# Attention and two expert stages in fp32 on one core: the q and k transposes of later units move from TensorE to VectorE

## The chip, the cores and the metric

The kernel runs on one core of one Trainium2 chip. Times are device microseconds of one execution; the number to predict is the median of the runs of the changed kernel. TensorE is PE, its weight loads PEld, VectorE is DVE, ScalarE ACT, GpSimd POOL; SP issues nearly all transfers.

## What is computed

```python
def _attn_ref(q, k, v, n_sink, window):        # (4, 8, 768, 64), 4 sinks, window 128
    scores = scale * np.matmul(q, k.transpose(0, 1, 3, 2))
    rel = pos[:, None] - pos[None, :]
    keep = (pos[None, :] < n_sink) | ((rel >= 0) & (rel < window))
    scores = np.where(keep, scores, -1e9)
    a = np.exp(scores - max); a = a / (sum + 1e-9)
    return np.matmul(a, v)

x = attn_out.transpose(0, 2, 1, 3).reshape(3072, 512)
x = ((x @ w1) * (x @ w2)) @ w3 @ w_out          # w's in float64, 1024 wide
e = argmax(x @ w_gate + bias[modality])         # 8 experts, top 1
out = gate[:, None] * (relu(x @ ew1[e]) @ ew2[e])
```

Everything is float32. Where the kernel needs nearly float32 accuracy from TensorE it splits an operand into a high part (rounded by ScalarE) and a low part (the difference) and adds three products.

## The kernel before

**Units and pairs.** The 3,072 tokens are 12 units of 256 tokens (4 batches, 3 units each; `c` is the unit's place in its batch). Attention works on one unit and one pair of heads at a time: 12 x 4 = 48 items, counted by `n`. On the 128 partitions lie the 2 x 64 head dimensions of the pair, or 128 tokens.

**One item of attention.** `a_load(n)` (L345) brings q and k, 128 tokens by 128 numbers each, in four transfers (L354). `a_tqk(n)` (L383) transposes the four 128x128 blocks on PE into the one PSUM bank of the pool `ps_t` (L392, L396). ScalarE writes the high parts from that bank, q to `qh` (L401) and k into a ring of three key blocks per pair (L402); one tick later `low_parts` writes the low parts, on DVE (L413, L415), for the first 8 items on PE and ACT. At the first unit of a batch POOL copies the four sink keys in front of each block of the ring (L421), so that a block is 4 + 128 columns wide. `a_scores(n, j)` (L427), for the two halves j of 128 queries, makes the scores in PSUM (L443), and DVE merges the two key blocks by a mask (L450 to L458) and takes the row maximum (L461); ACT takes the exponential with the row sum (L463) into `P`, which has the 4 sink columns ahead of the 128 window columns for each head. `norm` (L466) divides on DVE (L475). `a_sk` (L480) copies the sink columns of both heads side by side with ACT (L488); `a_skT` (L492) transposes them on PE (L499) into the one bank of `ps_x`. `a_pt` (L508) transposes the four window blocks of P on PE (L515), again into the bank of `ps_t`; ACT copies them out (L519, L521) and POOL keeps a triangle of each (L524). `a_pv` (L529) multiplies with v (L543, L546) and leaves the high part to ACT (L549), the low part to DVE (L554).

**The dense stages around it.** `moe1_stream` runs six groups of two units: per group eight pairs of 24 matmuls of 512 columns (L715) and pieces of six (L703) with the product of `w3` and `w_out`. Routing (`route`, L766) is DVE work, 16 reductions of 512 elements per unit (L776). The second expert stage follows attention, from about 620 us on.

**What sets the order.** `att_stream` (L562) yields steps, and `front` (L1005) takes them while it walks the dense stages; in each item the step order is:

```python
a_load(n + 2); a_scores(n, 0); yield
a_load_v(n); a_sk(n - 1); a_pt(n - 1); yield
a_tqk(n + 1); a_skT(n - 1); yield
a_scores(n, 1); yield
a_pv(n - 1); yield
```

From this program order a scheduler builds each engine's fixed queue at compile time. Each engine, SP too, then runs its queue in order, and an instruction that waits holds all behind it. The tiles qn and kn have two buffers each, so the load of item n + 2 waits for the last reader of item n.

Of the kernel before, what the change touches and what calls it, by code (L numbers as in the profile page):

```python
# [27 lines left out]
def attention_moe_moe_kernel(ctx, tc, q, k, v, w1, w2, w3, w_out, mod_id, w_gate, mod_bias, e_w1, e_w2, out,  # L28
                             n_sink, window, dbg=None):
    nc = tc.nc  # L30
# [17 lines left out]
    QDIV = float(D) ** 0.5  # L48
    FEW = 2 * NP if math.frexp(QDIV)[0] == 0.5 else 0
# [295 lines left out]
    def a_load(n):  # L345
        u, p = divmod(n, NP)
        b, c = divmod(u, NC)
        hs = slice(2 * p, 2 * p + 2)
        qn = att.tile([128, 2, 2 * D], F32, tag="qn", bufs=2, name="qn")
        kn = att.tile([128, 2, 2 * D], F32, tag="kn", bufs=2, name="kn")  # L350
        for src, dst in ((q, qn), (k, kn)):
            for j in range(2):
                s0 = c * UNIT + j * 128
                nc.sync.dma_start(out=dst[:, j].rearrange("p (h d) -> p h d", h=2),  # L354
                                  in_=src[b, hs, s0:s0 + 128, :].rearrange("h s d -> s h d"))
        nat[n] = (qn, kn)
# [26 lines left out]
    def a_tqk(n):  # L383
        u, p = divmod(n, NP)
        b, c = divmod(u, NC)
        qn, kn = nat.pop(n)
        if n < NP:
            ring.append(att.tile([128, 2, 3, KW], F32R, tag=f"ring{p}", bufs=1, name="ring"))
# [3 lines left out]
        tp = ps_t.tile([128, 4, 128], F32, tag="t", name="tqk")  # L392
        for x, src in enumerate((qn, kn)):
            for j in range(2):
                i = j if x == 0 or s0 < s1 else 1 - j
                nc.tensor.matmul(out=tp[:, 2 * x + i], lhsT=src[:, j], rhs=idf, is_transpose=True, start=(x + j == 0),  # L396
                                 stop=(x + j == 2), skip_group_check=True)
        qh = att.tile([128, 2, 128], F32R, tag="qh", bufs=2, name="qh")
        ql = att.tile([128, 2, 128], F32R, tag="ql", bufs=2, name="ql")
        scale = 1.0 / float(D) ** 0.5  # L400
        nc.scalar.activation(out=qh, in_=tp[:, 0:2], func=ACTF.Copy, scale=scale)  # L401
        nc.scalar.activation(out=kr[:, 0, blocks, NS:KW], in_=tp[:, 2:4], func=ACTF.Copy)  # L402

        def low_parts():
            if n < FEW:
                nc.tensor.matmul(out=tp[:, 0:2], lhsT=negq_r, rhs=qh, start=False, stop=True, skip_group_check=True)
                nc.tensor.matmul(out=tp[:, 2:4], lhsT=neg_r, rhs=kr[:, 0, blocks, NS:KW], start=False, stop=True,
                                 skip_group_check=True)
                nc.scalar.activation(out=ql, in_=tp[:, 0:2], func=ACTF.Copy, scale=scale)
# [3 lines left out]
            nc.vector.scalar_tensor_tensor(out=ql, in0=tp[:, 0:2], scalar=scale, in1=f32(qh), op0=ALU.mult,  # L413
                                           op1=ALU.subtract)
            nc.vector.tensor_tensor(out=kr[:, 1, blocks, NS:KW], in0=tp[:, 2:4], in1=f32(kr[:, 0, blocks, NS:KW]),  # L415
                                    op=ALU.subtract)
            sinks()

        def sinks():
            if c == 0:  # L420
                nc.gpsimd.tensor_copy(out=kr[:, :, :, 0:NS],  # L421
                                      in_=f32(kr[:, :, 0, NS:2 * NS]).unsqueeze(2).to_broadcast([128, 2, 3, NS]))

        stt["low", n] = defer(low_parts)
        stt["q", n] = (qh, ql)

    def a_scores(n, j):  # L427
# [12 lines left out]
        for i, (a, b_) in enumerate(((qh, 0), (ql, 0), (qh, 1))):  # L440
            for h in range(2):
                hp = slice(h * D, (h + 1) * D)
                nc.tensor.matmul(out=sp[:, h, 0:nk].rearrange("p (a b) -> p a b", b=KW), lhsT=a[hp, j, :],  # L443
                                 rhs=kr[hp, b_, blocks, :], start=(i == 0), stop=(i == 2))
        if j == 0:
            stt["p", n] = att.tile([128, 2, 2, KW], F32, tag="P", bufs=2, name="P")
        P = stt["p", n]
# [5 lines left out]
        else:  # L453
# [3 lines left out]
            if c == 0:  # L457
                nc.vector.copy_predicated(out=sp[:, :, 0:NS], mask=sk1_i.unsqueeze(1).to_broadcast([128, 2, NS]),  # L458
                                          data=negc.unsqueeze(1).to_broadcast([128, 2, NS]))
        lo = NS if blk0 else 0  # L460
        nc.vector.reduce_max(out=st[:, 0], in_=sp[:, :, lo:KW], axis=AXX, negate=True)  # L461
        for h in range(2):
            nc.scalar.activation(out=P[:, j, h, lo:KW], in_=sp[:, h, lo:KW], func=ACTF.Exp,  # L463
                                 bias=st[:, 0, h:h + 1], accum_out=st[:, 1, h:h + 1])

        def norm():  # L466
# [3 lines left out]
            if n < FEW:  # L470
                for h in range(2):
                    nc.scalar.activation(out=P[:, j, h, lo:KW], in_=P[:, j, h, lo:KW], func=ACTF.Copy,
                                         scale=r[:, h:h + 1])
                return
            nc.vector.tensor_tensor(out=P[:, j, :, lo:KW], in0=P[:, j, :, lo:KW],  # L475
                                    in1=r.unsqueeze(2).to_broadcast([128, 2, KW - lo]), op=ALU.mult)
# [3 lines left out]
    def a_sk(n):  # L480
        u, p = divmod(n, NP)
        b, c = divmod(u, NC)
        P = stt["p", n]
        for j in range(2):
            stt.pop(("norm", n, j))()
        j0 = 0 if c else 1
        skn = att.tile([128, 2, 2 * NS], F32, tag="skn", bufs=2, name="skn")
        nc.scalar.activation(out=skn[:, j0:2].rearrange("p j (h k) -> p j h k", h=2), in_=P[:, j0:2, :, 0:NS],  # L488
                             func=ACTF.Copy)
        stt["skn", n] = skn  # L490

    def a_skT(n):  # L492
        c = n // NP % NC
        skn = stt.pop(("skn", n))
# [3 lines left out]
        for j in range(0 if c else 1, 2):  # L498
            nc.tensor.transpose(out=xp[0:2 * NS, 1, j * 128:(j + 1) * 128], in_=skn[:, j], identity=idf)  # L499
# [8 lines left out]
    def a_pt(n):  # L508
        u, p = divmod(n, NP)
        b, c = divmod(u, NC)  # L510
        P = stt.pop(("p", n))
        tp = ps_t.tile([128, 4, 128], F32, tag="t", name="pt")
        for j in range(2):
            for h in range(2):
                nc.tensor.transpose(out=tp[:, 2 * j + h, :], in_=P[:, j, h, NS:KW], identity=idf)  # L515
# [13 lines left out]
    def a_pv(n):  # L529
# [25 lines left out]
        stt.pop(("q", n))  # L555
# [6 lines left out]
    def att_stream():  # L562
# [5 lines left out]
        for n in range(NN):  # L568
# [18 lines left out]
        a_sk(NN - 1); a_pt(NN - 1); yield  # L587
        a_skT(NN - 1)
# [641 lines left out]
```

## Time and profile before

| | us |
|---|---|
| runs | 990.64, 990.67, 991.0 (median 990.67) |
| the profiled execution's own time | 990.5 |
| its span, first to last instruction | 988.5 |
| busy: PE, DVE, ACT, POOL | 955.5, 634.0, 442.1, 161.0 |

An engine is busy while one of its instructions runs; durations of matmuls overlap, so the distance between two starts is what a matmul takes of PE, not its duration. A busy PE is not PE at its peak. The profile's line numbers are those of the code above.

### The profile page before, as it was taken

Reading aid. Unit: us, or ns where it says so; the run is one execution under the profiler, and the core shown is the slowest. Engines: PE = TensorE matmul, PEld = TensorE weight load, DVE = VectorE, ACT = ScalarE, POOL = GpSimd, SP = SyncE. Lnnn points to the kernel's source line nnn. Section 1 sums busy time; section 2 is a strip of 40 time slices with the busy share of each in tenths; the row PEclk is TensorE's granted clock in tenths of the full one; section 3 lists DMA queues with packets and bytes.
Section 4 is the critical chain, followed back from the end, with each engine's and each line's share of the span. In section 5 each row is a group of like instructions: output and inputs, shape, how many; then the busy total and the mean of one; then the engine's idle time right before and its main releaser. Section 6 shows DMA issues by size and latency. Waiting matters only on the chain. (4 is left out here: it accounts for less than half of the span.)

```text
span 988.5 us, 15433 instructions
## 1 busy us (share of the span) xinstructions
PE 955.5 (97%) x5000; PEld 728.4 (74%) x5000; DVE 634.0 (64%) x1913; ACT 442.1 (45%) x1266; POOL 161.0 (16%) x237
## 2 busy tenths in 40 slices
PE   4899999999999999999999999999999999999995
PEld 3667777767776777677767776787888888888884
DVE  7956994599449953995499538939934373443432
ACT  3687763454335433553355335413434334433433
POOL 1111110111112111111111111123130312211010
PEclk9899999999999999999999999999999999999998
DMA  8754724122212221221022210422455465444331
GB/s 255 237 159 137 224 73 124 29 54 62 46 28 46 64 46 25 51 73 42 19 54 69 47 23 10 138 76 55 141 180 115 150 78 167 149 144 135 106 121 51
DMA packets 125409, 93.99 MB, mean 95 GB/s; under 512 B 96711, under 2 KB 105159, under 8 KB 125200
## 3 DMA queue, kind: packets, MB, share of 16 engines
q1 hardware_dynamic: 120560, 80.12, 30.2%
q0 software_dynamic: 4768, 12.88, 4.1%
q8 instruction: 40, 0.66, 0.3%
q14 instruction: 41, 0.34, 0.2%
HBM read 80.14 MB, written 13.09 MB: 94 GB/s over the span
## 5 line engine op out<-in xcount | busy, mean ns | idle before, releaser
L715 PE MATMUL ab<-xb,wab 128*128 128x512 f32 x1152 | 288.5, 397 | 0.0
L715 PEld LDWEIGHTS ab<-xb,wab 128*128 128x128 f32 x1152 | 209.9, 188 | 44.6 <-DVE xb L554 0.2
L961 PE MATMUL x<-w 128*128 128x512 f32 x600 | 141.0, 392 | 0.0
L776 DVE CUSTOM_DVE_ANT_0 junk<-rows,wgb 128x512 bf16<-128x512 f32 x192 | 137.0, 714 | 1.9 <-ACT rows L763 0.5
L703 PE MATMUL x2p<-w3o,gh 128*128 128x512 f32 x384 | 130.1, 416 | 0.5 <-ACT gh L692 0.5
L961 PEld LDWEIGHTS x<-w 128*128 128x128 f32 x600 | 111.6, 188 | 23.1 <-DVE w L201 0.4
L524 POOL TENSOR_SCALAR_AFFINE_SELECT ptp<-ptf 128x512 f32<-128x512 f32 (+1 forms) x96 | 63.6, 687 | 344.9 <-ACT ptf L519 344.9
L463 ACT ACTIVATE P<-sp,st 128x132 f32<-128x132 f32 (+1 forms) x192 | 69.2, 366 | 67.6 <-DVE st L461 62.4
L201 DVE TENSOR_TENSOR w<-wst,w 128x512 fp32r<-128x512 f32 x112 | 71.3, 685 | 10.8 <-ACT w L200 10.8
L703 PEld LDWEIGHTS x2p<-w3o,gh 128*128 128x128 f32 x384 | 65.7, 189 | 16.2 <-ACT gh L692 2.8
L703 PE MATMUL x2p<-w3o,gl 128*128 128x512 f32 x192 | 76.5, 399 | 0.0
L722 DVE TENSOR_TENSOR g<-ab,bs 128x256 f32<-128x256 f32 x48 | 20.3, 423 | 85.6 <-PE tqk L396 49.0
L924 PE MATMUL ab<-w,w 128*128 128x512 f32 x288 | 74.9, 395 | 0.0
L928 DVE SCALAR_TENSOR_TENSOR w<-ab,w 128x512 fp32r<-128x512 f32 x48 | 33.1, 690 | 64.4 <-ACT w L927 64.2
L924 PE MATMUL ab<-w 128*128 128x512 f32 x288 | 73.6, 391 | 0.0
L692 ACT ACTIVATE gh<-g 128x256 fp32r<-128x256 f32 x96 | 39.7, 415 | 73.8 <-DVE g L722 55.7
L200 ACT ACTIVATE w<-wst 128x512 fp32r<-128x512 f32 x112 | 63.3, 628 | 7.4 <-DMA wst<-in_moe_w_dram 7.2
L443 PE MATMUL sp<-ring,qh 64*128 64x264 f32 (+1 forms) x384 | 62.7, 331 | 3.6 <-ACT P L463 3.5
L924 PEld LDWEIGHTS ab<-w,w 128*128 128x128 f32 x288 | 53.9, 188 | 12.4
L924 PEld LDWEIGHTS ab<-w 128*128 128x128 f32 x288 | 54.1, 188 | 12.1
L443 PEld LDWEIGHTS sp<-ring,qh 64*128 64x128 f32 x384 | 37.5, 185 | 34.6 <-issue 15.1
L927 ACT ACTIVATE w<-ab 128x512 fp32r<-128x512 f32 x48 | 28.7, 597 | 71.8 <-PE ab L924 71.4
(201 smaller groups left out, 1430.8 us busy)
## 6 DMA issues: line engine op xcount, KB each, us to landing
wst<-in_moe_w_dram SPq DMA_DIRECT2D x56, 512.0 KB
f64st<-in_moe_w_dram SPq DMA_DIRECT2D x32, 512.0 KB
vn<-in_v_dram SPq DMA_DIRECT2D x128, 64.0 KB
xs<-rows SPq DMA_DIRECT2D x12, 513.0 KB
qn<-in_q_dram SPq DMA_DIRECT2D x96, 64.0 KB
kn<-in_k_dram SPq DMA_DIRECT2D x96, 64.0 KB
f64st<-in_moe_w_out_dram SPq DMA_DIRECT2D x8, 512.0 KB
wgb<-wgt SPq DMA_DIRECT2D x1, 2048.0 KB
```

The source lines that it names most:

```text
L200: nc.scalar.activation(out=hi, in_=src, func=ACTF.Copy)
L201: lo_eng.tensor_tensor(out=lo, in0=src, in1=f32(hi), op=ALU.subtract)
L443: nc.tensor.matmul(out=sp[:, h, 0:nk].rearrange("p (a b) -> p a b", b=KW), lhsT=a[hp, j, :], rhs=kr[hp, b_, blocks, :], start=(i == 0), st ...
L463: nc.scalar.activation(out=P[:, j, h, lo:KW], in_=sp[:, h, lo:KW], func=ACTF.Exp, bias=st[:, 0, h:h + 1], accum_out=st[:, 1, h:h + 1])
L524: nc.gpsimd.affine_select(out=parts[:, a, i0:2].rearrange("p j h q -> p (j h) q"), in_=full[:, 2 * i0:4], pattern=[[0, 4 - 2 * i0], [sign, ...
L692: nc.scalar.activation(out=gh, in_=g, func=ACTF.Copy)
L703: nc.tensor.matmul(out=x2p[t], lhsT=a[:, sl], rhs=b_, start=(f == 0 and i == 0), stop=(f == KF - 1 and i == 2))
L715: nc.tensor.matmul(out=bank[nm].rearrange("p (u t) -> p u t", u=2), lhsT=a, rhs=b_, start=(kk == 0 and i == 0), stop=(kk == KD - 1 and i = ...
L776: nc.vector.tensor_tensor_reduce(out=junk, in0=rows[:, t, 0:DM], in1=wgb[0][:, e, :], scale=1.0, scalar=0.0, op0=ALU.mult, op1=ALU.add, ac ...
L924: nc.tensor.matmul(out=hp, lhsT=a[:, fs], rhs=b_, start=(kk == 0 and i == 0), stop=(kk == KD - 1 and i == 2))
L928: nc.vector.scalar_tensor_tensor(out=h[:, 1], in0=hp, scalar=0.0, in1=f32(h[:, 0]), op0=ALU.max, op1=ALU.subtract)
L961: nc.tensor.matmul(out=op, lhsT=a[:, ts], rhs=b_, start=(f == 0 and i == 0), stop=(f == KF - 1 and i == 2))
```

## The change

Items from n = 8 on (`BY_PE`) load q and k in blocks of 32 tokens by 32 dimensions: eight transfers instead of four, each to 32 partitions, in runs of 128 bytes instead of 256. One instruction of DVE, in place, turns all 32x32 blocks of q and k, which gives what PE's four transposes gave; ACT and DVE then read the parts from that tile in SBUF and not from PSUM. The first 8 items still use PE.

The ring's blocks get the sink keys a second time at their end (two copies on POOL instead of one). Head 0 reads window then sinks, head 1 sinks then window, so that in P the sinks of both heads lie side by side in columns 128 to 135. The ACT copy of the sinks goes, the sinks are transposed straight out of P, and this step comes right behind the transposes of P.

```diff
-        qn = att.tile([128, 2, 2 * D], F32, tag="qn", bufs=2, name="qn")
-        kn = att.tile([128, 2, 2 * D], F32, tag="kn", bufs=2, name="kn")
...
+        qk = att.tile([128, 2, UNIT], F32, tag="qk", bufs=2, name="qk")
+        for x, src in enumerate((q, k)):
+            if n < BY_PE:
...
+            for g in range(4):
+                h, d0 = 2 * p + g // 2, g % 2 * 32
+                nc.sync.dma_start(out=qk[g * 32:(g + 1) * 32, x].rearrange("p (b i) -> p b i", i=32),
+                                  in_=src[b, h, c * UNIT:(c + 1) * UNIT, d0:d0 + 32].rearrange("(b s) i -> s b i", s=32))
...
+        else:
+            nc.vector.transpose(out=qk.rearrange("p x s -> p (x s)"), in_=qk.rearrange("p x s -> p (x s)"))
+            qt, kt = (qk[:, x].rearrange("p (j s) -> p j s", j=2) for x in range(2))
+            if s0 > s1:
+                kt = kt[:, ::-1]
...
-        nc.scalar.activation(out=qh, in_=tp[:, 0:2], func=ACTF.Copy, scale=scale)
-        nc.scalar.activation(out=kr[:, 0, blocks, NS:KW], in_=tp[:, 2:4], func=ACTF.Copy)
+        nc.scalar.activation(out=qh, in_=qt, func=ACTF.Copy, scale=scale)
+        nc.scalar.activation(out=kr[:, 0, blocks, NS:KW], in_=kt, func=ACTF.Copy)
...
-                nc.gpsimd.tensor_copy(out=kr[:, :, :, 0:NS],
-                                      in_=f32(kr[:, :, 0, NS:2 * NS]).unsqueeze(2).to_broadcast([128, 2, 3, NS]))
+                for s0 in (0, KW):
+                    nc.gpsimd.tensor_copy(out=kr[:, :, :, s0:s0 + NS],
+                                          in_=f32(kr[:, :, 0, NS:2 * NS]).unsqueeze(2).to_broadcast([128, 2, 3, NS]))
...
+                c0 = (1 - h) * NS
+                nc.tensor.matmul(out=sp[:, h, c0:c0 + nk].rearrange("p (a b) -> p a b", b=KW), lhsT=a[hp, j, :],
+                                 rhs=kr[hp, b_, blocks, c0:c0 + KW], start=(i == 0), stop=(i == 2))
...
+            nc.tensor.transpose(out=xp[0:2 * NS, 1, j * 128:(j + 1) * 128], in_=P[:, j, 128:128 + 2 * NS], identity=idf)
...
-                a_sk(n - 1); a_pt(n - 1); yield
+                a_pt(n - 1); a_skT(n - 1); yield
             if n + 1 < NN:
                 a_tqk(n + 1)
-            if n:
-                a_skT(n - 1)
```

Where the queues change: first PE, in a stretch at the end of a dense group (about 301 to 304 us before). Line numbers below are each kernel's own. Before:

```order
L515 MATMUL pt<-idf,P 128x128 x4
L703 MATMUL x2p<-w3o,gh 128x512 x2
L703 MATMUL x2p<-w3o,gl 128x512
L703 MATMUL x2p<-w3o,gh 128x512 x2
L703 MATMUL x2p<-w3o,gl 128x512
L396 MATMUL tqk<-idf,qn 128x128 x2
L396 MATMUL tqk<-idf,kn 128x128 x2
L499 MATMUL xp<-idf,skn 8x128 x2
L703 MATMUL x2p<-w3o,gh 128x512 x2
L443 MATMUL sp<-ring,qh 128x264 x2
```

The same place with the change:

```order
L527 MATMUL pt<-idf,P 128x128 x4
L712 MATMUL x2p<-w3o,gh 128x512
L509 MATMUL xp<-idf,P 8x128 x2
L712 MATMUL x2p<-w3o,gh 128x512
L712 MATMUL x2p<-w3o,gl 128x512
L712 MATMUL x2p<-w3o,gh 128x512 x2
L712 MATMUL x2p<-w3o,gl 128x512
L712 MATMUL x2p<-w3o,gh 128x512 x2
L458 MATMUL sp<-ring,qh 128x264 x2
```

The four transposes of q and k are gone, and those of the sinks stand one matmul behind the transposes of P.

Then DVE, between the products g of the first and second column block of the next group. Before:

```order
L468 TENSOR_SCALAR st<-st 128x2
L776 ISA junk,lg<-rows,wgb 128x512
L776 ISA lg 128x1
L469 RECIPROCAL st<-st 128x2
L776 ISA junk,lg<-rows,wgb 128x512
L776 ISA lg 128x1
L475 TENSOR_TENSOR P<-P,st 128x2x128
L776 ISA junk,lg<-rows,wgb 128x512
```

With the change:

```order
L497 TENSOR_TENSOR P<-P,st 128x264
L796 CAST oh<-wk 128x16
L802 RECIPROCAL sm<-sm 128x2
L407 STREAM_TRANSPOSE qk<-qk 128x512
L470 COPY_PREDICATED sp<-past_i,negc 128x2x124
L803 COPY rows<-sm 128x2
L785 ISA junk,lg<-rows,wgb 128x512
L785 ISA lg 128x1
L484 TENSOR_REDUCE st<-sp 128x2
L428 TENSOR_TENSOR ring<-qk,ring 128x2x128
```

A block transpose (L407) has come in. From the last g of the group before to its first g the queue of DVE held 22 routing reductions (junk) and now holds 19 and three block transposes; in the next three blocks there were 7, 3 and 0 reductions and are 4, 7 and 2.

Last SP, at one of the routing stores xs; the brackets are the semaphores waited for. Before:

```order
L795 DMA xs<-rows 128x2x513 [waits DMAHW1_49,DVE_49,Activation_49]
L354 DMA qn<-in_q_dram 128x2x64 [waits DMAHW2_49,PE_49]
L354 DMA qn<-in_q_dram 128x2x64 [waits DMAHW3_49]
L354 DMA kn<-in_k_dram 128x2x64 [waits DMAHW4_49,PE_49]
L354 DMA kn<-in_k_dram 128x2x64 [waits DMAHW5_49]
L365 DMA vn<-in_v_dram 128x2x64 [waits DMAHW6_49,PE_49]
```

With the change:

```order
L804 DMA xs<-rows 128x2x513 [waits DMAHW1_49,DVE_49]
L360 DMA qk<-in_q_dram 32x8x32 [waits DMAHW2_49,DVE_49]
L360 DMA qk<-in_q_dram 32x8x32 [waits DMAHW3_49]
L360 DMA qk<-in_q_dram 32x8x32 [waits DMAHW4_49]
L360 DMA qk<-in_q_dram 32x8x32 [waits DMAHW5_49]
L360 DMA qk<-in_k_dram 32x8x32 [waits DMAHW6_49]
```

The load of q and k now waits for DVE (the low parts) where it waited for PE (the transposes), and has eight issues.

## Rows read from the trace of the kernel before

**Rows 1.** Page, parts 1 and 2: busy us (share) xinstructions, then forty slices of the span.

```profile
PE 955.5 (97%) x5000; PEld 728.4 (74%) x5000; DVE 634.0 (64%) x1913; ACT 442.1 (45%) x1266; POOL 161.0 (16%) x237
...
DVE  7956994599449953995499538939934373443432
PEclk9899999999999999999999999999999999999998
```

**Rows 2.** Windows of 50 us: length, busy us (x instructions) by engine, granted clock, DMA share, GB/s.

```profile
250.00:300.00 50.00, 50.00 (x274) 37.73 (x272) 23.63 (x78) 18.19 (x58) 7.81 (x10) 1.00 0.16 25
300.00:350.00 50.00, 48.71 (x289) 34.72 (x288) 47.17 (x168) 25.90 (x95) 8.85 (x14) 1.00 0.24 57
```

**Rows 3.** Timeline of PE alone: start us, duration, engine, line, operation, output and inputs.

```profile
302.79 0.38 PE L396 MATMUL tqk<-idf,qn 128*128 128x128 f32 x2
303.01 0.38 PE L396 MATMUL tqk<-idf,kn 128*128 128x128 f32 x2
303.22 0.38 PE L499 MATMUL xp<-idf,skn 128*8 128x128 f32 x2
303.36 0.71 PE L703 MATMUL x2p<-w3o,gh 128*128 128x512 f32 x2
...
311.06 0.44 PE L396 MATMUL tqk<-idf,qn 128*128 128x128 f32 x2
...
393.08 0.38 PE L396 MATMUL tqk<-idf,qn 128*128 128x128 f32 x2
...
393.51 0.38 PE L499 MATMUL xp<-idf,skn 128*8 128x128 f32 x2
```

**Rows 4.** Groups with shapes apart, q and k transposes on PE: x count | busy us, mean ns | idle.

```profile
L396 PE MATMUL tqk<-idf,qn 128*128 128x128 f32 x96 | 19.8, 285 | 0.1
L396 PE MATMUL tqk<-idf,kn 128*128 128x128 f32 x96 | 18.7, 276 | 0.0
```

**Rows 5.** Waits of PE, its weight loads, from 100 to 620 us: total us, times, longest.

```profile
PEld tqk L396 <- ACT ptf L519: 2.6, 8, 0.5
...
PEld tqk L396 <- ACT ptp L521: 1.8, 5, 0.4
```

**Rows 6.** Groups with shapes apart, VectorE: a block transpose and others of its width.

```profile
L752 DVE STREAM_TRANSPOSE wgst<-wgst 32x512 f32<-32x512 f32 x1 | 0.7, 692 | 0.0
...
L201 DVE TENSOR_TENSOR w<-wst,w 128x512 fp32r<-128x512 f32 x112 | 71.3, 685 | 10.8 <-ACT w L200 10.8
...
L776 DVE CUSTOM_DVE_ANT_0 junk<-rows,wgb 128x512 bf16<-128x512 f32 x192 | 137.0, 714 | 1.9 <-ACT rows L763 0.5
```

**Rows 7.** Windows of 10 us, columns as in Rows 2.

```profile
320.00:330.00 10.00, 9.00 (x57) 5.86 (x58) 9.88 (x40) 6.05 (x25) 2.20 (x4) 1.00 0.19 43
330.00:340.00 10.00, 10.00 (x57) 7.61 (x56) 9.87 (x37) 4.71 (x18) 1.61 (x3) 1.00 0.32 93
```

**Rows 8.** Timeline of VectorE: the low part of k for the unit transposed at 302.79.

```profile
306.79 0.42 DVE L415 TENSOR_TENSOR ring<-tqk,ring 128x256 fp32r<-128x256 f32 x1
```

**Rows 9.** Groups with shapes apart: ScalarE by source, its sink copies, and the copy of sink keys.

```profile
L401 ACT ACTIVATE qh<-tqk 128x256 fp32r<-128x256 f32 x48 | 18.4, 384 | 44.2 <-PE tqk L396 43.6
...
L692 ACT ACTIVATE gh<-g 128x256 fp32r<-128x256 f32 x96 | 39.7, 415 | 73.8 <-DVE g L722 55.7 <-PE x2p L703 16.8 <-DVE gl L693 1.0
...
L488 ACT ACTIVATE skn<-P 128x16 f32<-128x16 f32 x32 | 6.9, 215 | 21.1 <-DVE P L475 18.9 <-DVE wk L783 1.6 <-DVE cwork L163 0.6
...
L421 POOL CAST ring<-ring 128x24 fp32r<-128x24 f32 x16 | 4.1, 254 | 66.2 <-ACT ring L410 30.8 <-DVE ring L415 13.8 <-DVE sp L458 12.3
```

**Rows 10.** DMA view from 250 to 300 us, SP timeline there, SP waits of the span.

```profile
q1 hardware_dynamic: 4923, 1.20, 14.9%
...
257.14 0.89 SPq L354 DMA_DIRECT2D qn<-in_q_dram  x2
258.12 0.94 SPq L354 DMA_DIRECT2D kn<-in_k_dram  x2
...
SPq L795 <- DVE rows L794: 47.3, 9, 23.7
```

More of the change, by code (lines that the diff above doesn't have):

```diff
@@ L391, in a_tqk @@
         blocks = slice(s0, s1 + 1) if s0 < s1 else slice(s1, s0 + 1, s0 - s1)
[L392 to L397, printed above, removed]
+        if n < BY_PE:
+            tp = ps_t.tile([128, 4, 128], F32, tag="t", name="tqk")
+            for x in range(2):
+                for j in range(2):
+                    i = j if x == 0 or s0 < s1 else 1 - j
+                    nc.tensor.matmul(out=tp[:, 2 * x + i], lhsT=qk[:, x, j * 128:(j + 1) * 128], rhs=idf, is_transpose=True,
+                                     start=(x + j == 0), stop=(x + j == 2), skip_group_check=True)
+            qt, kt = tp[:, 0:2], tp[:, 2:4]
+        else:
[3 more added lines that the diff above has]
+                kt = kt[:, ::-1]
         qh = att.tile([128, 2, 128], F32R, tag="qh", bufs=2, name="qh")
@@ L442, in a_scores, with both @@
                 hp = slice(h * D, (h + 1) * D)
-                nc.tensor.matmul(out=sp[:, h, 0:nk].rearrange("p (a b) -> p a b", b=KW), lhsT=a[hp, j, :],
-                                 rhs=kr[hp, b_, blocks, :], start=(i == 0), stop=(i == 2))
+                c0 = (1 - h) * NS
+                nc.tensor.matmul(out=sp[:, h, c0:c0 + nk].rearrange("p (a b) -> p a b", b=KW), lhsT=a[hp, j, :],
+                                 rhs=kr[hp, b_, blocks, c0:c0 + KW], start=(i == 0), stop=(i == 2))
         if j == 0:
-            stt["p", n] = att.tile([128, 2, 2, KW], F32, tag="P", bufs=2, name="P")
-        P = stt["p", n]
+            stt["p", n] = att.tile([128, 2, 2 * (KW + NS)], F32, tag="P", bufs=2, name="P")
+        P = stt["p", n][:, j]
+        flat = sp.rearrange("p h c -> p (h c)")
+        def both(first, step, n_):
+            return flat[:, first:first + 2 * step].rearrange("p (h c) -> p h c", h=2)[:, :, 0:n_]
         st = att.tile([128, 3, 2], F32, tag="st", bufs=6, name="st")
@@ L471, in norm @@
                 for h in range(2):
[L472 to L473 removed]
+                    nc.scalar.activation(out=rows[:, h], in_=rows[:, h], func=ACTF.Copy, scale=r[:, h:h + 1])
                 return
[L475 to L476 removed]
+            nc.vector.tensor_tensor(out=rows, in0=rows, in1=r.unsqueeze(2).to_broadcast([128, 2, KW - (NS if blk0 else 0)]),
+                                    op=ALU.mult)
         stt["norm", n, j] = defer(norm)
[L480 to L490, printed above, removed]
     def a_skT(n):
         c = n // NP % NC
[L494 removed]
+        P = stt["p", n]
         xp = ps_x.tile([128, 2, 256], F32, tag="x", name="xp")
@@ L510, in a_pt @@
         b, c = divmod(u, NC)
-        P = stt.pop(("p", n))
+        P = stt["p", n]
+        for j in range(2):
+            stt.pop(("norm", n, j))()
         tp = ps_t.tile([128, 4, 128], F32, tag="t", name="pt")
@@ L514, in a_pt @@
             for h in range(2):
[L515 removed]
+                nc.tensor.transpose(out=tp[:, 2 * j + h, :], in_=P[:, j, h * (KW + NS):h * (KW + NS) + 128], identity=idf)
         full = att.tile([128, 4, 128], F32, tag="ptf", bufs=1, name="ptf")
```

38 lines of the change are left out of this document (20 added, 18 removed).

## The prediction

> **What bounds the kernel now.** The first view is the page. PE is busy for 97% of the span and its slices read 9 nearly throughout, while VectorE is at 64% with slices that swing between 3 and 9 [rows 1]. The granted clock is full (the 2.4 GHz level) from the second slice on, so no time is to be had from the clock. A share of 64% is an average, so the second view is the windows: in the window of 250 to 300 us PE is busy for all 50.00 us and VectorE for 23.63, and in the next one PE for 48.71 and VectorE for 47.17 [rows 2]. The kernel alternates between stretches where PE alone sets the pace and stretches, around the end of each dense group, where VectorE has almost no room either: 9.88 and 9.87 of 10 us [rows 7]. There are five such ends with attention in them between 190 and 610 us, one per group. So what comes off PE is gained one for one in the first kind of stretch; in the second kind it is gained only if VectorE does not become later. That is the question here, since the change takes work from PE and gives work to VectorE.
>
> **What it removes.** From item 8 on, 40 items, PE loses four transposes each, 160 in all. What one set costs is read from starts, since durations overlap: from the first q transpose at 302.79 to the sink transposes that follow them at 303.22 is 0.43 us, and from 393.08 to 393.51 again 0.43 [rows 3]. So 40 x 0.43 = **17.2 us** off PE. The other way to price it is the busy time of the group, 19.8 + 18.7 = 38.5 us for 192 transposes [rows 4], 160/192 of which is 32 us; but that counts the drain of each set, under which the next matmuls have begun (the second pair lasts 0.38 us, yet the next row starts 0.21 after it). I take the 17.2 and keep the 32 as the far end of the gain.
>
> The transposes also share one PSUM bank with those of P, and PE waited for ACT to empty it: 2.6 us in 8 waits and 1.8 us in 5 between 100 and 620 us, where all 40 items lie [rows 5]. With q and k out of this bank that is **4.4 us** less. Below, the end is nothing, if the matmul that moves up waits for something else that is late.
>
> On this the Trainium skill, page "VectorE: DVE Perf Modes", speaks twice. Its section "The three transpose paths" gives 390 ns for a 128x128 bf16 block on TensorE and 311 on VectorE; by an estimate from its 390, 40 sets of four would be 62 us of PE, and the time about 924. The rows, 0.43 us for four in a row, decide against that figure. Its section "Rules for kernel authors" would leave a 128x128 transpose on TensorE where PSUM will do, which speaks against the change; what that would cost here is the first rival below.
>
> **What it adds to VectorE.** 40 block transposes, 512 columns on 128 partitions. The trace has one on 32 partitions, 692 ns; other instructions of 512 columns on 128 partitions take 685 to 714 [rows 6], so partitions do not seem to matter. 40 x 0.69 = 27.7 us, on an engine with 64% busy. On the path I cost them at nothing, and the cover is this: the routing reductions (0.714 us each, [rows 6]) are needed only much later and fill the queue wherever there is room. In the queue printed above the saturated stretch loses three reductions (2.1 us) and gains three block transposes (2.1 us), and the reductions come back in the next three column blocks, in the part of the group where VectorE was idle for half the time [rows 2]. If that cover is gone, it costs 5 ends x 3 x 0.69 = 10 us.
>
> **What is hidden anyway.** ACT loses 48 sink copies of some 0.21 us, and pays for reading 80 operands from SBUF: 415 ns against 384 from PSUM [rows 9], 2.5 us in all; at 45% busy both are nothing. POOL copies sink keys twice, 16 x 0.254 us = 4.1 us more [rows 9], in front of the scores of a batch's first unit; I take 0 and keep 4 as the bad end. Scores, maximum, exponential and division keep their sizes.
>
> **What is moved.** The sink transposes follow those of P almost at once, so the bank that they write must already be free: the low part of the item before (DVE, L554) must have been read from it. Before, four q and k transposes and four more matmuls stood between. No row shows this wait on the new place. Below it is nothing; above it is the longest wait for the other bank, 0.5 us [rows 5], in each of some 20 items near group ends, 10 us. Nearest is that bank's average, 4.4/13 = 0.34 us; in one of four such items that is 5 x 0.34 = **1.7 us**, which I take. Behind the waiting transposes all of PE's queue stands.
>
> **The loads.** Eight issues at 0.46 us each (four took 0.89 + 0.94 us, [rows 10]) are 3.7 us of SP. From 250 to 300 us 4,923 packets, nearly all of 256 bytes, took 14.9% of 16 engines, 24 ns each [rows 10]. An item's 2,048 packets of 128 bytes are then between 1.5 us (by bytes) and 6.2 (twice as long each); at 24 ns, 3.1 us. Issue and packets one after the other are 6.8 us. The buffer is now free only after the low parts: 307.2 for the item transposed at 302.79 [rows 3, 8], 4.4 us later than before. Items follow at 8.3 us there (302.79, 311.06, [rows 3]), so from that moment to the block transpose two items on are 2 x 8.3 - 4.4 = 12.1 us. It fits, and costs nothing.
>
> **The sum**, against the profiled execution (990.5 us, span 988.5, that is 0.17 below the median of the runs): 990.5 - 17.2 - 4.4 + 1.7 = 970.6, in round numbers **970.5 us**.
>
> **Rivals.**
> *VectorE sets the pace at the group ends.* Then the four or so items of each end (20 of 40) save PE work without shortening anything, and half of the bank waits stay: 990.5 - 8.6 - 2.2 = about 980. For it: 9.88 of 10 us [rows 7]. Against it: three reductions leave just there, and PE was busy for 48.71 of 50 us in the same window. If the reductions that leave are not those that were in the way, the 10 us above are added, and it is 990, no change.
>
> *The block transpose waits for its load, and VectorE with it* (the side that ends slower). The load now waits for VectorE, and a store of routing rows, itself waiting for VectorE, stands ahead of the loads on SP: such stores held SP for 47.3 us in 9 waits, 23.7 us at the longest [rows 10]. A block transpose at the head of VectorE's queue then stops maxima, divisions and low parts, and PE next. It decides where the time from the store's release to the block transpose is under some 7 us. At 1 us lost by PE per item the sum is 970.5 + 40 = about 1,010, and above half a microsecond per item the kernel is slower than before. Against it are the 12.1 us, and that SP's long waits were for buffers that nobody needed yet. The Trainium skill, "DMA: Bandwidth & Descriptors", section "Specifications", says that transfers under 512 bytes are read, modified and written and miss the line rate, which speaks for it; the runs before, of 256 bytes, were under this limit too, and nothing here shows the step from 256 to 128.
>
> *Nothing is gained*, because the matmuls that move up wait for the exponentials of the scores ahead of them: about 990. Against it: PE has dense matmuls between in most places.
>
> *More is gained*: with PE's drains counted (the 32 us), about 960.
>
> **How the numbers follow.** Forecast 0.70 (its own range 964 to 979); VectorE's pace 0.14 (975 to 988); late loads 0.07; nothing 0.05; more 0.04. Under 962 lies little of the last, over 984 the second half of the late cases, so 962 to 984 holds a bit over 8 in 10. A measurement can tell 0.2%, 2 us, from no change: faster is 0.70 + 0.04 + 0.13 = 0.87, the same 0.05, slower 0.08.
>
> **What would show it.** Right: no q and k transposes after the first 8 items; PE busy about 18 us less with the idle time near what it was; block transposes of about 0.69 us; VectorE near 660 us busy, with the reductions spread over more column blocks; SP's waits for VectorE without a wait of VectorE for the loads. Wrong: waits of VectorE for q or k transfers, PE's sink transposes waiting for the low part of the item before, or windows at the group ends where VectorE is full and PE idle for over 2 us.

## The result and the profile after

The changed kernel takes **975.64 us** (median of 975.31, 975.55, 975.73 and 977.43) against 990.67 before, a ratio of 0.985 with a 95% interval of 0.9838 to 0.9862. The forecast was 970.5 with a range of 962 to 984, so the sign and the range hold, and 15.0 us were gained where 20 were forecast. Three quarters of the forecast came; the experiments ask where the other 5 us are.

The page of the changed kernel, parts 1 and 2, answers to [rows 1]:

```profile
PE 932.9 (96%) x4840; PEld 709.7 (73%) x4840; DVE 651.8 (67%) x1953; ACT 440.5 (45%) x1218; POOL 167.2 (17%) x253
...
DVE  7956996699659964896599649929934374333422
...
PEclk9999999999999999999999999999999999999998
```

PE has exactly the 160 instructions less, and 22.6 us less of busy time. The span fell by only 14.7 us (988.5 to 973.8), so PE now stands idle for 40.9 us where it was 33.0: **7.9 us of new idle time**. The clock is at its 2.4 GHz level as before, and has no part in it.

The windows say where the idle time is (length, busy us by engine, clock, DMA share, GB/s; the first four answer to [rows 2, 7]):

```profile
250.00:300.00 50.00, 49.84 (x276) 37.00 (x276) 28.25 (x94) 19.93 (x60) 9.91 (x14) 1.00 0.21 39
300.00:350.00 50.00, 45.87 (x269) 33.12 (x265) 47.66 (x173) 24.20 (x86) 7.93 (x14) 1.00 0.27 53
320.00:330.00 10.00, 8.97 (x53) 6.38 (x54) 9.57 (x43) 4.95 (x18) 2.19 (x4) 1.00 0.27 44
330.00:340.00 10.00, 10.00 (x54) 7.54 (x54) 9.90 (x33) 4.09 (x17) 1.50 (x2) 1.00 0.35 83
290.00:350.00 60.00, 55.72 (x324) 39.24 (x322) 56.07 (x201) 30.00 (x105) 9.58 (x16) 1.00 0.27 52
```

The last line of these has this counterpart in the kernel before:

```profile
290.00:350.00 60.00, 58.71 (x341) 41.41 (x339) 54.09 (x188) 30.78 (x109) 10.07 (x16) 1.00 0.22 52
```

In the long stretch of this dense group PE is full, or nearly so, in both. Around the group's end, 290 to 350 us, PE was idle for 1.29 us and is now idle for 4.28, and VectorE went from 54.09 to 56.07 of 60. The five ends are not alike. Counted from the copy of a group's eighth column block to that of the next group's second, PE's idle time grew by 0.3, 1.6, 1.4, 0.3 and 0.3 us; another 1.4 us lie behind the second end, at 349 us, and 1.0 in the first group. The moved work itself is as forecast (groups of VectorE from 90 to 610 us: xcount | busy us, mean ns | idle before, and what ended it):

```profile
L785 DVE CUSTOM_DVE_ANT_0 junk<-rows,wgb 128x512 bf16<-128x512 f32 x148 | 105.5, 713 | 1.6 <-ACT rows L772 0.9
...
L407 DVE STREAM_TRANSPOSE qk<-qk 128x512 f32<-128x512 f32 x40 | 28.3, 708 | 10.7 <-DMA vn<-in_v_dram 7.6 <-DMA qk<-in_k_dram 2.4 <-issue 0.6
```

A block transpose takes 708 ns against the 692 on 32 partitions of [rows 6], so four times the partitions made 2% of difference. But VectorE waited some 10 us for the loads ahead of it, which the forecast had at nothing. What PE waited for from 295 to 350 us (total us, times, longest):

```profile
PE pt L527 <- DVE P L497: 2.0, 2, 1.0
PE pt L527 <- DVE wk L814: 1.4, 1, 1.4
PE xp L555 <- POOL ring L435: 0.6, 1, 0.6
PE sp L458 <- ACT P L486: 0.2, 1, 0.2
```

The first two are transposes of P that wait for VectorE. The third is a product with v behind GpSimd's copies of the sink keys, of which the change makes twice as many. From 195 to 610 us PE's transposes of P waited for VectorE for 1.0 us before and wait for 4.7 now. Before:

```profile
PE pt L515 <- DVE P L475: 1.0, 3, 0.3
```

and now:

```profile
PE pt L527 <- DVE P L497: 3.3, 5, 1.0
...
PE pt L527 <- DVE wk L814: 1.4, 1, 1.4
```

The two longest can be followed step by step. PE's timeline of the first:

```profile
311.67 0.44 PE L527 MATMUL pt<-idf,P 128*128 128x128 f32 x2 [0.95 <-DVE P L497]
```

and VectorE's, from the step on the row sum (L491) to the division of P (L497):

```profile
308.87 0.68 DVE L785 CUSTOM_DVE_ANT_0 junk<-rows,wgb 128x512 bf16<-128x512 f32 x1
...
309.82 0.17 DVE L491 TENSOR_SCALAR st<-st 128x2 f32<-128x2 f32 x1
310.19 0.71 DVE L407 STREAM_TRANSPOSE qk<-qk 128x512 f32<-128x512 f32 x1 [0.20 <-DMA vn<-in_v_dram]
310.83 0.12 DVE L492 RECIPROCAL st<-st 128x2 f32<-128x2 f32 x1
...
311.19 0.43 DVE L497 TENSOR_TENSOR P<-P,st 128x264 f32<-128x264 f32 x1
```

A block transpose stands between the row sum and its reciprocal; with its wait of 0.20 us it takes about as long as PE waits. PE's timeline of the second:

```profile
347.21 0.17 PE L811 MATMUL rk<-oh,ones_bf 128*128 128x8 bf16 x1
...
349.59 0.63 PE L527 MATMUL pt<-idf,P 128*128 128x128 f32 x4 [1.39 <-DVE wk L814]
```

and VectorE's, of the same stretch:

```profile
345.59 0.69 DVE L785 CUSTOM_DVE_ANT_0 junk<-rows,wgb 128x512 bf16<-128x512 f32 x1
...
346.99 0.71 DVE L407 STREAM_TRANSPOSE qk<-qk 128x512 f32<-128x512 f32 x1 [0.20 <-issue]
...
347.82 0.42 DVE L497 TENSOR_TENSOR P<-P,st 128x256 f32<-128x256 f32 x1
...
348.38 0.42 DVE L428 TENSOR_TENSOR ring<-qk,ring 128x256 fp32r<-128x256 f32 x1
...
349.08 0.15 DVE L812 TENSOR_TENSOR wk<-rk,dec 128x16 f32<-128x16 f32 x1
...
349.36 0.17 DVE L814 TENSOR_TENSOR wk<-wk,dec 128x16 f32<-128x16 f32 x1
```

The routing ranks `rk` lie in the same PSUM bank as the transposes of P. They are written by 347.4, but VectorE reads them only from 349.08 on, since a block transpose, the division of P and a low part are ahead in its queue. The bank that q and k no longer use is here held up by VectorE's queue, and the moved work is part of that queue.

To place the gain, the starts of the 48 copies of column blocks (six groups of eight; L719 before, L728 after) are compared. They mark PE's progress through the program. In the last group PE has no attention left, and the distance stays: 671.90 to 656.98 us, a lead of 14.9. Of it 6.1 us were won inside the groups and 8.8 at the five group ends, counted as above; counted only to the first copy of the next group the ends have 14.0, so the split depends on the cut. This **lead of the last block** is used below, since it can also be read where routing is altered. It comes from one profiled execution of each kernel.

### The profile page after: what moved, and what is told of

It is laid out like the page before. It is cut to its first block, busy times and chain, and to the rows that moved or that the text cites. A ratio compares the mean times of both kernels' runs of the same rounds, so it can differ in the third digit from the quotient of the medians.

```text
span 973.8 us, 15418 instructions
## 1 busy us (share of the span) xinstructions
PE 932.9 (96%) x4840; PEld 709.7 (73%) x4840; DVE 651.8 (67%) x1953; ACT 440.5 (45%) x1218; POOL 167.2 (17%) x253
## 5 line engine op out<-in xcount | busy, mean ns | idle before, releaser
L536 POOL TENSOR_SCALAR_AFFINE_SELECT ptp<-ptf 128x512 f32<-128x512 f32 (+1 forms) x96 | 66.5, 716 | 308.0 <-ACT ptf L531 308.0
L933 PEld LDWEIGHTS ab<-w 128*128 128x128 f32 x288 | 54.1, 188 | 12.1
L974 POOL DMA_INDIRECT out_dram<-late,ti x25 | 25.2, 1009 | 203.9 <-ACT late L973 166.6
```

What stands on the lines that cost most here:

```text
L536: nc.gpsimd.affine_select(out=parts[:, a, i0:2].rearrange("p j h q -> p (j h) q"), in_=full[:, 2 * i0:4], pattern=[[0, 4 - 2 * i0], [sign, ...
L933: nc.tensor.matmul(out=hp, lhsT=a[:, fs], rhs=b_, start=(kk == 0 and i == 0), stop=(kk == KD - 1 and i == 2))
```

## The experiments

| kernel | median us | ratio to before, 95% | lead of the last block, us |
|---|---|---|---|
| the changed kernel | 975.64 | 0.9838 to 0.9862 | 14.9 |
| three buffers for q and k | 972.67 | 0.9792 to 0.9829 | 17.5 |
| sink transposes at their old place | 976.13 | 0.9828 to 0.9865 | 14.4 |
| all transposes by PE | 992.23 | 1.0006 to 1.0025 | -4.0 |
| more VectorE work | 973.78 | 0.9803 to 0.9841 | 16.5 |
| stores on ACT's queue | 975.17 | 0.9829 to 0.9864 | 15.0 |
| three buffers, low part on GpSimd | 978.59 | 0.9859 to 0.9892 | 12.1 |
| reductions later | 973.79 | 0.981 to 0.9842 | 16.8 |
| reductions later, three buffers | 973.22 | 0.9802 to 0.9834 | 16.8 |
| reductions later, ranks later | 975.0 | 0.9821 to 0.9854 | 14.4 |

In the row with all transposes by PE the lead of -4.0 belongs to an execution of 994.49 us, one of three near 994.4 among ten; the other seven lie between 991.7 and 992.7.

**1. Are the loads late?**

```diff
-        qk = att.tile([128, 2, UNIT], F32, tag="qk", bufs=2, name="qk")
+        qk = att.tile([128, 2, UNIT], F32, tag="qk", bufs=3, name="qk")
```

(To make room, v has two buffers for three, and the small statistics tile four for six.)

> The tile of q and k gets three buffers instead of two, so that the load of item n + 2 no longer waits for the low parts of item n (to make room, v has two buffers instead of three and the row statistics four instead of six). If late loads are the missing 5 us (VectorE stood 10.2 us at the block transpose until a transfer had landed), the time falls from 975.6 to about 971 and VectorE's waits for q, k and v transfers vanish. If VectorE's own load at the group ends is the cause, the time stays within 1.5 us of 975.6 although those waits vanish. If the earlier sink step is, no change either.

Measured 972.67, 3.0 us better than the changed kernel, and the best of those that compute the whole result. It lies between the two expectations. Block transposes wait 4.0 us for loads instead of 10.0. In the window from 290 to 350 us PE is idle for 2.95 us and not 4.28:

```profile
290.00:350.00 60.00, 57.05 (x332) 40.72 (x332) 56.81 (x203) 30.92 (x106) 8.97 (x17) 1.00 0.28 58
```

That the loads cause the 3 us does not follow: runs 2 and 4 wait longer for loads and are not slower, and the same edit took buffers from v and from the statistics.

**2. Does the place of the sink transposes cost anything?**

```diff
-                a_pt(n - 1); a_skT(n - 1); yield
+                a_pt(n - 1); yield
...
+            if n:
+                a_skT(n - 1)
```

> Only the place of the sink transposes is undone: they stand again behind the step that prepares q and k of the next item. If the missing 5 us come from the sink step (VectorE stood 21.8 us in 16 waits at the low part of the sinks until ScalarE had written the high part, a wait that the kernel before hardly had), the time falls to about 971 to 972 and that wait to a few us. If late loads or VectorE's load are the cause, the time stays within 1.5 us of 975.6.

Measured 976.13, the same. The new wait of VectorE for ACT's copy of the sinks, 18.7 us in 13 waits in the changed kernel, is down to 2.4, and PE gains nothing by it: it was a wait of an engine with time to spare. The block transposes wait 15.3 us for loads here, without loss.

**3. The sink half alone.**

```diff
-    BY_PE = 2 * NP
+    BY_PE = NU * NP
```

> Only the other half of the change: all 48 items load and transpose q and k as before (PE), the sinks stay side by side and in one burst. The forecast's working gives 990.5 + 1.7 = 992 for this, and so 16 to 17 us for the move of the transposes; if the sink half alone costs 4 us or more, it is 995 or above; if the sink half gains by itself (no copy on ScalarE), it is below 989.

Measured 992.23, 0.15% over before. In its profiled execution the blocks run 4 us behind from the first one on (126 us in the kernel before) and lose nothing later, so over the 40 items the sink half is worth nothing. The gain belongs to the transposes of q and k.

**4. Does VectorE's total load set the pace?**

```diff
+            for _ in range(2):
+                nc.vector.transpose(out=qk[:, 0], in_=qk[:, 0])
```

Two more transposes per item, which undo one another.

> Each of the 40 block transposes is preceded by two more of half its width that undo each other: some 40 x 0.75 = 30 us more on VectorE, nothing else. If VectorE has room and only late loads and waits cost, the time rises by less than 5 us (under 981). If VectorE sets the pace at the group ends, about half of the 40 fall there and the time rises by 10 to 15 us (986 to 991).

VectorE's group of the added transposes, from 90 to 610 us:

```profile
L408 DVE STREAM_TRANSPOSE qk<-qk 128x256 f32<-128x256 f32 x80 | 34.8, 435 | 17.0 <-DMA qk<-in_q_dram 9.4 <-DMA qk<-in_k_dram 6.9
```

Measured 973.78: 1.9 us faster with more work and longer waits for loads. From 290 to 350 us PE idles for 2.30 us, less than the 4.28 of the changed kernel, beside a VectorE that is fuller (56.69 us):

```profile
290.00:350.00 60.00, 57.70 (x333) 40.72 (x332) 56.69 (x195) 30.73 (x105) 8.16 (x16) 1.00 0.26 52
```

So neither VectorE's total nor the waits for loads set the time by themselves, and a VectorE without room at the group ends is not enough to explain PE's idle time. A scheduler builds the queues anew for each kernel; that this order is what gained here is the likeliest reason, and not shown by itself. **Differences of about 2 us between two builds can then be the order alone**, which limits all that follows.

**5. Where VectorE's work lies: short reductions, a pair.** Three quarters of each routing dot product are left out, in the kernel before and in the changed one:

```diff
-                nc.vector.tensor_tensor_reduce(out=junk, in0=rows[:, t, 0:DM], in1=wgb[0][:, e, :], scale=1.0,
+                nc.vector.tensor_tensor_reduce(out=junk[:, 0:128], in0=rows[:, t, 0:128], in1=wgb[0][:, e, 0:128], scale=1.0,
```

> Leaves out three quarters of every routing dot product (columns 128 to 511), in the kernel before; the routing then comes out otherwise, so that only the time up to the last attention block (copies of the six groups' column blocks) is compared, not the total. It frees VectorE at the group ends of about 0.45 us per reduction. It is one half of a pair with the next run. If VectorE's load at the group ends held the kernel before up, its own blocks come earlier than before's by 2 us or more in all at the end of group 5; if PE alone set the pace there, by under 1 us.

> The same three quarters of every routing dot product left out, in the changed kernel. Two theories of the 5 us that the forecast has too much. (a) VectorE's load at the group ends took them: with the reductions short, the column blocks of the last group lie about 20 us earlier than in the pair's other half (17.2 + 4.4 less about 1.5 for the sink copies), where 14.9 was seen between the two whole kernels. (b) The late loads and the order took them: the pair differs by 14 to 16 us, as the whole kernels do, since no load comes earlier by this.

The start of the last block copy, in the kernel before with short reductions:

```profile
673.70 0.60 ACT L719 ACTIVATE bs<-ab 128x512 f32<-128x512 f32 x1 [3.44 <-DVE dri L836]
```

and in the changed kernel with short reductions:

```profile
652.12 0.60 ACT L728 ACTIVATE bs<-ab 128x512 f32<-128x512 f32 x1 [3.44 <-DVE dri L845]
```

The lead within the pair is **21.6 us**, where the whole kernels show 14.9 (one execution of each half). The kernel before does not profit from short reductions: its last block comes 1.8 us later, which neither expectation allowed for, and PE's idle time over the span rises from 33.0 to 35.6 us. The changed one comes 4.9 us earlier, none of it by the end of the first two groups, 3.4 by the end of the third. The window at the start of that stretch:

```profile
290.00:350.00 60.00, 58.21 (x338) 41.71 (x336) 48.09 (x204) 31.21 (x108) 8.86 (x20) 1.00 0.29 61
```

VectorE is at 48.09 of 60 us, and PE idles for 1.79 us instead of 4.28. The number of theory (a) came. Three things keep it from being shown: 1.8 of the 21.6 us are a loss of the kernel before, so that against the whole kernel before the lead is 19.8; the block transposes wait only 4.0 us for loads here, where theory (b) took for granted that no load comes earlier; and most of the gain comes from one stretch and not from all five ends. Run 10 bears on this again.

**6. The store out of the way of the loads.**

```diff
-        nc.sync.dma_start(out=xs[u * UNIT:(u + 1) * UNIT, :].rearrange("(t p) d -> p t d", p=128), in_=rows)
+        nc.scalar.dma_start(out=xs[u * UNIT:(u + 1) * UNIT, :].rearrange("(t p) d -> p t d", p=128), in_=rows)
```

> The store of a unit's rows is issued from ACT's queue and not from SP's, so that no load of q or k stands behind it. If the stores ahead of the loads made them late (the three buffers' gain was 3.0 us), the time falls to 973 to 974, and the waits of block transposes for loads shrink from some 10 us to under 3. If the loads are late because the buffer comes free late, it stays within 1 us of 975.6. ACT waits for VectorE's rows at each store; at worst that holds up its exponentials, and the time rises over 977.

Measured 975.17, the same; the block transposes still wait 8.3 us for loads. The queue on which a store is issued is not what makes them late, and ACT's part in it costs nothing.

**7. Three buffers, and a low part for GpSimd.** The edit of run 1, and:

```diff
-            nc.vector.tensor_tensor(out=kr[:, 1, blocks, NS:KW], in0=kt, in1=f32(kr[:, 0, blocks, NS:KW]),
+            nc.gpsimd.tensor_tensor(out=kr[:, 1, blocks, NS:KW], in0=kt, in1=f32(kr[:, 0, blocks, NS:KW]),
```

> Three buffers for q and k as in the first experiment, and k's low part subtracted by GpSimd and not by VectorE (40 subtractions of 512 columns). VectorE is freed of about 0.5 us per item, 10 of them at group ends. If VectorE's pace at the ends is what is left of the missing time, the total falls from 972.7 to about 970 to 971; if it is not, it stays at 972 to 974; if the slower GpSimd makes k late for the scores, it rises to over 975.

Measured 978.59, 5.9 us worse than run 1. GpSimd takes twice VectorE's 0.42 us:

```profile
L428 POOL TENSOR_TENSOR ring<-qk,ring 128x256 fp32r<-128x256 f32 x40 | 32.9, 823 | 120.4 <-ACT ring L415 100.4 <-DMA qk<-in_q_dram 12.5 <-DMA vn<-in_v_dram 7.4
```

VectorE is not freed of what it hands over: 40 subtractions of 0.42 us are 16.8, but its page's busy time fell by 2.3 us only (653.6 to 651.3), since others of its instructions got longer (the low parts of q from 416 to 524 ns in the mean, the division of P from 433 to 466). How the 5.9 us come about is not shown.

**8. Reductions later, with nothing left out.** A small copy from a column block of the next group into the tile of the logits, which the reductions must follow, and a later place for them in the program, hold them back for four of the five groups:

```diff
+            late_bs[0] = bs
...
+        if late_bs[0] is not None:
+            nc.vector.tensor_copy(out=lg, in_=late_bs[0][:, 0:2 * E].rearrange("p (t e) -> p t e", t=2))
...
-                    due = min(t, 46000) / 1100
+                    due = (min(t, 46000) / 1100 if gr in (0, NU // 2 - 1)
+                           else max(0, min(t, 46000) - 4000) / 650)
+                if last or gr == 0:
+                    late_bs[0] = None
```

> The whole result is computed again. In the changed kernel the routing reductions of a group are held back by a copy that they have to follow: it reads a column block of the next group, so that they spread over that group's blocks (some 4, 5, 8, 6, 8 per block) where 19 of 32 lay at its end before. Total work of VectorE is the same (8 small copies more). If reductions in VectorE's queue at the group ends took the missing 5 us, the time falls from 975.6 to 969 to 971, as the pair with short reductions says. If what counted there was that the reductions were shorter in all, it stays within 1.5 us of 975.6; if the reductions now hold up the products of the column blocks, it rises.

Measured 973.79, a gain of 1.9 us of the 5, and a miss for the expectation. It is no larger than what run 4 gained with more work, and the waits for loads fell here too, from 10.0 to 3.7 us. The window shows the relief at the group's end:

```profile
290.00:350.00 60.00, 57.01 (x332) 40.98 (x331) 51.17 (x175) 29.80 (x105) 8.60 (x19) 1.00 0.26 52
```

but PE has a new wait, its longest from 195 to 610 us: the rank matmuls come before the late one-hot operand.

```profile
PE rk L810 <- DVE oh L799: 3.5, 4, 1.5
```

**9. Both together**, runs 1 and 8.

> The later reductions together with the three buffers for q and k. If the two are separate causes, their gains add: 3.0 us from the buffers on top, 966 to 968. If both treat the same idle time of PE at the group ends (a transpose that comes late, by its load or by the queue), it is 969 to 971 like the later reductions alone.

Measured 973.22, the same as run 8 and not better than run 1. The gains do not add, as the second expectation has it, though its number was missed.

**10. Three buffers with short reductions**, runs 1 and 5.

> Leaves out three quarters of every routing dot product, as the earlier pair did, now with the three buffers; compared by the start of the last group's last column block alone. Separate causes: 23 us or more ahead of the kernel before with short reductions. One cause: 21 to 22.5 us, as without the third buffer (21.6).

Its last block is 19.2 us ahead of the kernel before with short reductions, fewer than the 21.6 with two buffers. So a third buffer has nothing left to give beside short reductions, and costs 2.4 us, about what the order may do. The other way round holds as well: beside three buffers the short reductions give nothing, the last block starts at 654.36 us without them (run 1) and at 654.45 with them. PE's idle time from 290 to 350 us is 2.24 us, with far more room on VectorE than in run 4:

```profile
290.00:350.00 60.00, 57.76 (x336) 41.24 (x335) 47.39 (x204) 31.14 (x107) 7.70 (x18) 1.00 0.28 61
```

Neither expectation again. The result speaks against two separate causes, and also against VectorE's room as the one cause: 47.39 and 56.69 us of work on VectorE go with nearly the same idle time of PE.

**11. Reductions later, and the ranks later too.** Run 8 with the rank matmuls nine program steps after the store of the rows, and no longer one:

```diff
-        yield
+        for _ in range(9 if held else 1):
+            yield
         rk = ps_t.tile([128, 3, E], F32, tag="t", name="rk")
```

> The later reductions again, with two buffers for q and k, and the rank matmuls of the routing written nine steps further behind in the program, since PE waited 3.5 us for their one-hot operand in the run with the later reductions (973.8 us). If VectorE's queue at the group ends took the missing 5 us and these waits gave the gain back, the time falls to 969.5 to 971, and the last column block starts about 20 us earlier than in the kernel before (16.8 in the run with the later reductions, 14.9 in the changed kernel). If it stays within 1 us of 973.8, moving the reductions is worth only 2 us and the rest of what short reductions gave came from their length.

Measured 975.0, a miss. The waits for the one-hot operand are gone, and another thing took their place, once. VectorE's timeline:

```profile
375.20 0.42 DVE L484 TENSOR_REDUCE st<-sp 128x2 f32<-128x264 f32 x1
384.17 0.71 DVE L407 STREAM_TRANSPOSE qk<-qk 128x512 f32<-128x512 f32 x1 [8.54 <-DMA vn<-in_v_dram]
```

SP's, of the loads for this transpose:

```profile
368.72 0.37 SPq L808 DMA_DIRECT2D xs<-rows  x1
370.62 3.31 SPq L360 DMA_DIRECT2D qk<-in_q_dram  x4
373.98 1.94 SPq L360 DMA_DIRECT2D qk<-in_k_dram  x4
```

and PE's, behind it:

```profile
388.33 1.22 PE L712 MATMUL x2p<-w3o,gh 128*128 128x512 f32 x2 [4.45 <-ACT gh L701]
```

This is the second rival of the forecast, in one place: a block transpose stands at the head of VectorE's queue and waits for its load, the products of the column block wait behind it, ACT waits for them and PE for ACT. PE stood idle for 4.45 us, and the granted clock, 1.00 up to 385 us, was 0.50 from 387 to 389 us, the 1.2 GHz level. The lead was 9.5 us at the last block before it, and 4.9 at the next. Without that step the profiled execution (976.1 us) would be at about 976.1 - 4.6 = 971.5 and the median at 970.4, both estimates; the expectation was 969.5 to 971. Such an order without a late load was not tried.

The leads at the last block of each group, in us, bring the runs together:

| group | changed | three buffers | pair with short reductions | reductions later | and ranks later |
|---|---|---|---|---|---|
| 0 | 1.9 | 1.1 | 2.5 | 2.1 | 1.8 |
| 1 | 5.7 | 5.2 | 6.5 | 6.2 | 6.4 |
| 2 | 7.1 | 8.5 | 11.0 | 9.5 | 4.9 |
| 3 | 10.3 | 12.9 | 15.1 | 12.2 | 8.6 |
| 4 | 13.9 | 16.6 | 19.1 | 15.8 | 13.4 |
| 5 | 14.9 | 17.5 | 21.6 | 16.8 | 14.4 |

Where a kernel is ahead of the changed one at the end, more of that comes with group 2 than with any other.

## Why the prediction was right, and where it was 5 us off

**What bounds the kernel: right.** PE is full, or nearly so, inside the groups before and after, and the question was the group ends. Of the 7.9 us of new idle time 3.9 lie at the five ends and 1.4 just behind the second. Two of the three signs that the text named for being wrong did appear all the same: waits of VectorE for transfers (10 us), and a window at a group's end in which PE idles for over 2 us beside a nearly full VectorE (4.28 us). The range held with them.

**What it removes, 17.2 + 4.4 us: its sum fits, its two terms are not shown apart.** In the pair the lead is 21.6 us, which is this sum, and 19.8 against the whole kernel before; the order makes some 2 us uncertain, so that the exact match is luck. PE's busy time fell by 22.6 us. The waits of q's and k's transposes for ACT to empty the bank [rows 5] went with those transposes, but PE's weight loads wait longer for other things. From 100 to 620 us, before and now:

```profile
PEld sp L443 <- ACT P L463: 9.8, 22, 0.9
```

and

```profile
PEld sp L458 <- ACT P L486: 14.0, 31, 1.0
...
PEld sp L458 <- ACT gh L701: 4.9, 14, 0.4
```

So the low end that the text gave for the 4.4 us, that the matmul which moves up waits for something else, is not excluded. The price by starts (0.43 us a set, [rows 3]) fits the runs, and the 32 us by busy time do not. By the 390 ns of the Trainium skill ("VectorE: DVE Perf Modes", section "The three transpose paths") it would be 62 us, an estimate from that figure; no run comes near it.

**The wait for the sink transposes, +1.7: did not come.** PE's weight load waited once, for 0.2 us, for the low part of the item before, and the old place of the sinks gives the same time. The price was drawn from a neighbouring bank; here VectorE reads the low part early enough.

**VectorE's 27.7 us at nothing: the size was right, the nothing was not.** The work is 28.3 us. The cover was named as reductions that "fill the queue wherever there is room", of which three leave the stretch where three transposes come. But what is left in the queue still stands between PE's scores and its transposes of P, and the block transposes stand there too: one is directly ahead at 311 us and one in the row of work ahead at 349 us, where PE waits for 0.95 and 1.39 us. In all, PE's transposes of P wait 3.7 us longer for VectorE than before. That is what the traces show of the missing 5 us.

That more room on VectorE would bring the 5 us back is not shown. Short reductions bring 4.9 us with two buffers and none with three, and run 4 gains 1.9 us with less room. The text had bounded this term at 10 us if the cover is gone; the loss lies mostly at two of the five ends, and the time falls between the forecast and the first rival's 980.

The move of the transposes alone is worth 992.2 - 975.6 = 16.6 us. The Trainium skill, "VectorE: DVE Perf Modes", section "Rules for kernel authors", would leave a 128x128 transpose on TensorE where PSUM will do. The measurement goes the other way here.

**The loads at nothing: wrong in its reason, and not settled for the time.** The text had 12.1 us of room against 6.8 of need. In fact the block transposes waited 10 us in all for loads, once 5.2 us (at 465.91 us, where PE's weight loads waited 0.35 us for what came of it). Runs 2 and 4 have longer such waits and no loss, so most of a wait can be slack; in run 11 one wait cost PE 4.45 us. What is queued behind the transpose at that moment makes the difference between these two cases. The time of a load was also not one number (below).

**POOL's 4 us and ACT's sizes at nothing: nearly right.** POOL's busy time rose by 6.2 us, ACT's fell by 1.6, and run 3 shows no loss after the start. In the changed kernel PE waited once, for 0.6 us, behind the copies of the sink keys.

What stays open is how much of the missing 5 us is VectorE's lack of room, how much is late loads, and how much the order that the scheduler built. Three buffers, short reductions and later reductions each remove part of it, mostly at the same place, and do not add. A version that beats both kernels is run 1, at 972.67.

## What to carry to other kernels

Whether work that leaves the bounding engine for another one is gained in full cannot be read from that engine's mean share, here 67%: look at the stretch where both are near full, and then at which instructions of the receiving engine stand in front of what the bounding engine waits for. Work that isn't urgent (here the reductions) is a cover only if it gives way, and in a fixed queue it does not do so by itself; moving it made its own followers late (run 8). A result of one or two microseconds between two builds whose queues are ordered anew is not evidence for a mechanism; a lead that is read block by block is better.

## What was unexpected of the hardware

**Loads behind a store.** From 250 to 300 us the 9,248 packets of the queue took 20.7% of 16 engines, 18 ns each. From 450 to 466 us, where the first loads were issued 2.3 us after a 513 KB store, 2,992 packets took 96.7%, 83 ns each, the store's own among them. The first window has such a store too, but the next loads were issued 3.8 us after it (DMA view of the changed kernel, one window after the other):

```profile
q1 hardware_dynamic: 9248, 1.90, 20.7%
...
q1 hardware_dynamic: 2992, 0.92, 96.7%
```

The block transpose at 465.91 is the one that waited longest. The Trainium skill, "DMA: Bandwidth & Descriptors", section "Specifications", has transfers under 512 bytes read, modified and written. Apart from 256 packets of the store in each, the packets of both windows are under that, so it does not tell them apart, and no run here shows what does.

**VectorE beside GpSimd.** A reduction that takes 0.69 us took 1.12 when it began beside GpSimd's selection (timeline of the changed kernel):

```profile
304.15 1.86 POOL L536 TENSOR_SCALAR_AFFINE_SELECT ptp<-ptf 128x512 f32<-128x512 f32 x2 [6.37 <-ACT ptf L531]
...
304.39 1.12 DVE L785 CUSTOM_DVE_ANT_0 junk<-rows,wgb 128x512 bf16<-128x512 f32 x1
```

The Trainium skill, "SBUF — State Buffer", section "SBUF: two separate sides", says that a VectorE instruction with two SBUF inputs and a GpSimd one that reads SBUF exclude one another for the whole of an instruction. These rows, 1.12 us against 0.69, agree with it. So does run 7, where VectorE's two-input instructions grew as GpSimd took over subtractions: the low part of q, which the change itself made a reader of two SBUF tiles, took up to 1.03 us there against 0.42 as a rule.
